# Linear attention and a gated feed-forward block on one core: phi(K) from two values instead of three, first loads split by rows, new orders

## The chip, the core and the metric

The kernel runs on one NeuronCore of one Trainium2 chip. A core has TensorE (PE, matmuls and transposes; its weight loads are shown apart as PEld), VectorE (DVE), ScalarE (ACT), GpSimd (POOL) and SyncE (SP), which here only issues transfers (DMAs). Each engine runs its own instructions in a fixed order; semaphores order them against each other. Matmul results land in PSUM, eight banks of 512 float32 values per partition; everything else is kept in SBUF, 128 partitions.

The metric is the device time of one execution in microseconds, lower is better; the figure of a kernel is the median of several runs.

## The reference

All inputs are bfloat16; 2048 tokens, width 448, 16 heads of 28, inner width 1792.

```python
def _A_ref(x, wqkv, wo):                       # linear attention
    qkv = (x @ wqkv).reshape(B, S, 3, H, Dh).transpose(2, 0, 3, 1, 4)
    q, k, v = qkv[0], qkv[1], qkv[2]
    phi = lambda t: jnp.where(t > 0, t + 1, jnp.exp(t)) + 1e-6
    pq, pk = phi(q), phi(k)
    kv = jnp.einsum("bhsd,bhse->bhde", pk, v)
    z = jnp.einsum("bhsd->bhd", pk)
    num = jnp.einsum("bhqd,bhde->bhqe", pq, kv)
    den = jnp.einsum("bhqd,bhd->bhq", pq, z)[..., None] + 1e-6
    return (num / den).transpose(0, 2, 1, 3).reshape(B, S, D) @ wo

def _B_ref(x, w_gate, w_up, w_down):           # gated feed-forward
    return jnp.einsum("bsf,fd->bsd", _gelu(x @ w_gate) * (x @ w_up), w_down)

h = x + _A_ref(_layernorm(x), A_wqkv, A_wo)
return h + _B_ref(_layernorm(h), B_w_gate, B_w_up, B_w_down)
```

## The kernel before

The 2048 tokens are 16 tiles of 128. Tile t is row t of each partition's 16 consecutive tokens, so tiles 0 and 1 lie next to each other in memory for every partition.

**Stage 1, K and Q (lines 430 to 505).** For each tile VectorE makes the statistics (`bnst1_t`, `bnag1_t`, lines 413 and 414) and ACT the reciprocal deviation (`ln1_t`, `rstd1_t`). Tiles 0 to 3 are normed by VectorE (`normD_t`, line 435), transposed by TensorE (`tr0_t`, `tr1_t`, line 443) and copied out of PSUM in two halves, the first by ACT (`evxA_t`), the second by VectorE (`evxD_t`). Tiles 4 to 15 are normed by GpSimd (`normP_t`) and transposed by a DMA that SP issues (`xT_t`). The normed tile has 512 columns; the last 64 are ones, so the fourth of its four transposed blocks has 64 rows of data and 64 rows of ones. The weights' fourth block is padded with zero rows (line 364) to meet them.

`k_t` is four matmuls of 448 columns (line 469, the helper `proj`). `ek_t` is ACT's exponential of K; `ck_t` (line 481) caps it at 1 + 1e-6; `pk_t` (line 482) adds it to the maximum of K and 1e-6: that is phi(K). `pt4_t` (line 488; for tiles 10 to 15 `pt1_t` and `pt3_t`, one and three matmuls) adds the product of the normed tile and phi(K) up in PSUM banks 4 to 7 over all tiles: kv is later formed from this sum and the V weights, so V itself is never computed. The columns of ones make z in the lower half of bank 7. `q_t` is computed in the same way, with an exponential (`eq_t`) and a relu (`rq_t`) on ACT; `cq_t` and `aq_t` on VectorE finish phi(Q). K and Q share PSUM banks 0 to 3 in the order of `SEQ` (line 245), so that a projection can start when the readers of the fourth one before it are done: Q1 follows K1 in bank 2, K3 follows K0 in bank 1.

**The turn (lines 514 to 555).** `z1` (ACT) and `z0` (VectorE) take z out of PSUM. `evpA_0`, `evpA_1` (ACT) and `evpD_2`, `evpD_3` (VectorE) take the four sums out. `kv` (line 527) multiplies with the V weights, `kvm` masks the heads, `w2_c` (line 547) multiplies with the output weights, so that the attention's output of a tile is one product with `w2`.

**Stage 2 (lines 558 to 708).** Pairs of tiles: phi(Q) times z summed per head (`t1p_t`, `t1d_t`, `dr_t`), division, transpose, `out...`, residual `hr_t`, second norm, transpose. Then chunks of the feed-forward block: `gu..` (lines 731 and 733, gate and up in the two halves of the array), gelu on ACT (`ge..`), product on VectorE (`hm..`), `down..` (line 697) and the last residual.

**Order.** Nothing is reordered while the kernel runs. `ORDERS` lists, engine by engine, the tasks' numbers (a task's number is its place in the program text, counted from 0); `HOLD` says for a task that waits for several others which of the waits is issued first. Waits are derived from the buffers that tasks read and write; a wait that another one implies is dropped. The first loads are issued by SP and ACT (lines 364 to 377), before ACT's first table load; `warm` (line 407) is 40 matmuls of 128 columns on ones, ahead of everything else on TensorE.

The orders before, by names, up to what the prediction steps through:

```text
PE : warm tr0_0 tr1_0 tr0_1 tr1_1 k_0 tr0_2 tr1_2 k_1 q_0 tr0_3 tr1_3 k_2 k_3 pt4_0 q_1 pt4_1 pt4_2 q_2 k_4 ...
     k_14 pt3_10 k_15 pt1_11 pt3_11 pt1_12 pt1_13 pt3_12 pt1_14 pt1_15 pt3_13 pt3_14 pt3_15 q_5 q_4 kv q_7 q_8 w2_2 ...
DVE: wvpad wqkpad bnst1_0 bnag1_0 bnst1_1 bnag1_1 normD_0 bnst1_2 normD_1 bnag1_2 bnst1_3 evxD_0 bnag1_3 normD_2
     evxD_1 normD_3 evxD_2 bnst1_4 ck_0 bnag1_4 bnst1_5 pk_0 bnag1_5 evxD_3 ck_1 bnst1_6 pk_1 ...
     ck_15 pk_15 aq_3 cq_1 evpD_3 z0 aq_1 t1d_0 dr_0 evpD_2 rd_0 dr_1 dr_2 kvm ...
SP : dx0 dx2 dw1 dx4 dw1_t dx8 dx12 dwv dwv_t dwo xT_4 xT_5 xT_6 xT_8 xT_7 ...
ACT: dx1 dw0 dw0_t tbl1 ln1_0 rstd1_0 ln1_1 rstd1_1 evxA_0 ...
```

(`dxN` loads x from tile N, `dw0` the first 384 rows of the K weights, `dw0_t` the last 64, `dw1` and `dw1_t` the Q weights.)

Of the kernel before, what the change touches and what calls it, by code (L numbers as in the profile page):

```python
# [822 lines left out]
```

## Time and profile before

| | us |
|---|---|
| median of 3 runs | 190.3 |
| lowest, highest run | 190.28, 190.66 |
| span of the profiled execution, first to last instruction | 188.3 |

The profiled execution's own time is not given apart from its span; the 2.0 us between the span and the median are taken as what lies around the span.

How to read the rows. A row of a timeline has start and duration in us, the engine, the source line (of this listing), the operation, what it writes and reads, how many instructions are merged, and in brackets the engine's idle time before it and what ended it. A row of a group has count, busy time, mean ns of one, and idle time before. A row of a stage has its ends, its length, each engine's busy time and count, the granted clock, the DMA engines' share and GB/s. A row of a DMA issue has KB and the us from issue to landing; a row of a queue has packets, MB and share. The trace models the end of a matmul: a single one of 448 columns shows 350 ns, though the next can start much earlier, so the spacing of starts tells the pace.

### The profile page before, as it was taken

To read this page: it belongs to the slowest core of one execution; us is meant where nothing else is said; L and a number is where in the kernel's file an instruction comes from. 1 tells how busy PE (TensorE), PEld (TensorE's weight loads), DVE (VectorE), ACT (ScalarE), POOL (GpSimd) and SP (SyncE) were. 2 spreads that over 40 slices of the span, in tenths; PEclk is the share of its full clock that TensorE was granted. 3 is DMA by queue.
4 is the path that set the end of the run, shared out by engine and by line. 5 is a ranking of instruction groups with operands and counts; after the bars stand their busy time and mean duration, and the time that the engine had idled before them with its cause. 6 is when DMAs were issued, how large, how long until landed. Compare 5 with 4: busy or idle time off the path is not lost.

```text
span 188.3 us, 4459 instructions
## 1 busy us (share of the span) xinstructions
PE 184.3 (98%) x1813; PEld 109.2 (58%) x1813; DVE 129.3 (69%) x330; ACT 76.5 (41%) x220; POOL 50.0 (27%) x91
## 2 busy tenths in 40 slices
PE   7999999999999999999999999999999999999994
PEld 7545555555688788965554555555545545454554
DVE  4999959999899998786796762562645244335432
ACT  3878752799963231432234222321242222224100
POOL 6067910704505686033614000206100000000000
PEclk9999999999999999999999999999999999999999
DMA  5996458999393526820005720000096000002024
GB/s 169 387 231 88 96 104 194 218 222 174 65 320 64 95 52 116 84 52 0 0 3 98 144 54 0 0 3 2 3 135 111 3 0 24 3 0 98 3 79 140
DMA packets 35076, 17.11 MB, mean 91 GB/s; under 512 B 26864, under 2 KB 33648, under 8 KB 35056
## 3 DMA queue, kind: packets, MB, share of 16 engines
q1 hardware_dynamic: 34432, 16.32, 41.1%
q10 hardware_dynamic: 624, 0.52, 0.8%
q8 instruction: 14, 0.23, 0.5%
q14 instruction: 6, 0.05, 0.1%
HBM read 8.26 MB, written 1.84 MB: 54 GB/s over the span
## 4 chain that ended last, share of the span: by engine, by line
PE 94%; DVE 3%; DMA 1%; issue 0%
PE ps L733 38%; PE ps L697 19%; PE ps L469 12%; PE ps L731 9%; PE ps L488 6%; PE ps L627 3%; PE ps L678 3%; PE ps L628 2%; DMA x_sb<-in_A_x_dram 1%; DVE st L413 1%; PE ps L617 1%; PE ps L547 1%; PE ps L527 1%; PE ps L443 0%; PE ps L654 0%; DVE den L572 0%
## 5 line engine op out<-in xcount | busy, mean ns | idle before, releaser
L733 PE MATMUL ps<-hnT,wgu_sb 64*128 64x512 bf16 (+1 forms) x490 | 88.8, 333 | 0.0
L731 PE MATMUL ps<-hnT,wgu_sb 64*128 64x512 bf16 (+1 forms) x490 | 88.6, 333 | 0.0
L751 ACT ACTIVATE gl<-ps 128x256 bf16<-128x256 f32 x112 | 36.6, 383 | 85.3 <-PE ps L731 84.4
L753 DVE TENSOR_TENSOR hh<-ps,gl 128x256 bf16<-128x256 f32 x112 | 42.1, 416 | 41.4 <-ACT gl L751 41.3
L733 PEld LDWEIGHTS ps<-hnT,wgu_sb 64*128 64x128 bf16 x490 | 45.2, 94 | 32.9 <-DVE hh L753 3.4
L731 PEld LDWEIGHTS ps<-hnT,wgu_sb 64*128 64x128 bf16 x490 | 45.4, 94 | 2.5
L697 PE MATMUL ps<-wd_sb,hh 64*128 64x448 bf16 x392 | 41.5, 349 | 0.0
L697 PEld LDWEIGHTS ps<-wd_sb,hh 64*128 64x128 bf16 x392 | 23.2, 94 | 14.5
L469 PE MATMUL ps<-wqk_sb,xnT 128*128 128x448 bf16 x128 | 27.4, 353 | 0.0
L413 DVE BATCH_NORM_STATS2 st<-x_sb 128x6 f32<-128x448 bf16 x32 | 19.2, 612 | 1.8 <-DMA x_sb<-in_A_x_dram 1.7
L585 POOL TENSOR_TENSOR t<-pq,zbc 128x448 f32<-128x448 bf16 x12 | 12.3, 1042 | 23.7 <-DVE pq L583 22.0
L469 PEld LDWEIGHTS ps<-wqk_sb,xnT 128*128 128x128 bf16 x128 | 11.9, 98 | 11.4 <-DVE pk L482 0.8
L488 PE MATMUL ps<-pk,xnn 128*128 128x448 bf16 x64 | 13.9, 352 | 0.0
L627 PE MATMUL ps<-w,pqnT 64*128 64x448 bf16 x49 | 11.5, 349 | 0.1
L425 POOL TENSOR_SCALAR ln<-mv 128x2 f32<-128x2 f32 x7 | 2.0, 291 | 35.2 <-DVE mv L414 35.0
L480 ACT ACTIVATE e<-ps 128x448 bf16<-128x448 f32 x16 | 8.5, 539 | 5.6 <-PE ps L469 5.5
L628 PE MATMUL ps<-pt_sb,pqnT 64*128 64x448 bf16 x42 | 10.2, 350 | 0.0
L633 DVE TENSOR_TENSOR x_sb<-ps,x_sb 128x448 bf16<-128x448 f32 x16 | 9.6, 616 | 0.7 <-PE ps L628 0.6
L662 POOL TENSOR_SCALAR hn<-x_sb,nm,rs 128x448 bf16<-128x448 bf16 x14 | 9.9, 719 | 0.4
L482 DVE SCALAR_TENSOR_TENSOR pk<-ps,e 128x448 bf16<-128x448 f32 x16 | 9.8, 617 | 0.1
L488 PEld LDWEIGHTS ps<-pk,xnn 128*128 128x128 bf16 x64 | 6.3, 98 | 5.9 <-DVE pk L482 0.3
L453 POOL TENSOR_SCALAR xnn<-x_sb,nm,rs 128x448 bf16<-128x448 bf16 x12 | 8.9, 744 | 2.2 <-ACT rs L422 1.9
(85 smaller groups left out, 160.5 us busy)
## 6 DMA issues: line engine op xcount, KB each, us to landing
out_dram<-x_sb SPq DMA_DIRECT2D x15, 112.0 KB, 1.8
wd_sb<-in_B_w_down_dram SPq DMA_DIRECT2D x1, 1568.0 KB, 8.4
x_sb<-in_A_x_dram SPq DMA_DIRECT2D x3, 448.0 KB, 5.9
wgu_sb<-in_B_w_gate_dram SPq DMA_DIRECT2D x1, 896.0 KB, 12.1
wgu_sb<-in_B_w_up_dram SPq DMA_DIRECT2D x1, 896.0 KB, 16.5
wgu_sb<-in_B_w_gate_dram SPq DMA_DIRECT2D x1, 672.0 KB, 6.1
wgu_sb<-in_B_w_up_dram SPq DMA_DIRECT2D x1, 672.0 KB, 8.5
wo_sb<-in_A_wo_dram SPq DMA_DIRECT2D x1, 392.0 KB, 7.5
```

The source lines that it names most:

```text
L413: op("dve", lambda e: e.bn_stats(st[:, t, :], src_ap), [b_src], [b_st[t]], "bnst%s_%d" % (tag, t))
L469: ins = e.matmul(ps[:, bk, 0:D], xnT[:, t, k, :], wqk_sb[:, k, c0:c0 + D], start=(k == 0), stop=(k == 3))
L488: ins = e.matmul(ps[:, BK_PT[c], 0:D], xnn[:, t % XN_R, c * 128:(c + 1) * 128], pk[:, ip, :], start=(t == 0), stop=(t == T - 1))
L585: op("pool", lambda e, n=n: e.tensor_tensor(t1[:, n, :], pq[:, a + n, :], zbc[:, :], ALU.mult), [b_pq[a + n]] + b_z, [b_t1[n]], "t1p_%d" % ...
L627: e.matmul(ps[:, BK_OUT[0], 0:D], pqnT[ra, i2, sg // 2, :], w2[ra, sg // 2, :], start=(sg == 0), stop=(sg == 5))
L628: ins = e.matmul(ps[:, BK_OUT[1], 0:D], pqnT[rb, i2, 3 + (sg + 1) // 2, :], (w2 if sg == 6 else w2s)[rb, sg // 2, :], start=(sg == 0), sto ...
L662: op("pool", lambda e, t=t, sh=sh: e.tensor_scalar(hn[:, sh, 0:D], x_sb[:, t, :], nm2[:, t:t + 1], rs2[:, t:t + 1], ALU.add, ALU.mult), [b ...
L697: ins = e.matmul(ps[:, bko[half][n], 0:D], hh[rows, j, sl[n]], wd_sb[rows, j, :], start=(j == 0 and (half == 0 or p == 6)), stop=(j == NJ ...
L731: first = e.matmul(psG[:, jj * N:(jj + 1) * N], wgu_sb[A_, k, j * 128:(j + 1) * 128], hnT[A_, ka_, c0:c0 + N], start=(k == 0), stop=(k == ...
L733: ins = e.matmul(psU[:, jj * N:(jj + 1) * N], wgu_sb[B_, k, j * 128:(j + 1) * 128], hnT[B_, kb_, c0:c0 + N], start=(k == 0), stop=(k == NK ...
L751: G.add("act", lambda e, gi=gi, cs_=cs_, psG=psG: e.activation(gl[:, gi, cs_], psG[:, cs_], AF.Gelu_apprx_tanh), r=[b_ps[BK_G[i]]], w=[b_g ...
L753: op("dve", lambda e, dst=dst, srcU=srcU, srcL=srcL: e.tensor_tensor(dst, srcU, srcL, ALU.mult), [b_ps[BK_U[i]], b_glh], [b_ar[j_][t % HR] ...
```

## The change

- **phi(K).** Row 64 of the fourth block of the K weights, one of the zero rows that meet the ones, becomes 1 (`w1row`), so that the matmuls give K + 1. `ek_t` takes the exponential with bias -1. `ck_t` is gone; `pk_t` takes the minimum of the exponential and 1 and then the maximum with K + 1.
- **The 1e-6 of phi(K).** phi(K) gets a column more that holds 1e-6 (`pkeps`, set once), and the `pt` matmuls have 449 columns, so that 1e-6 times the column sums of the normed tiles is in column 448 of each bank. It is added when the sums are taken out: `ecol` copies two of these columns to SBUF for ACT's evictions, VectorE's evictions read theirs in PSUM. z gets 2048 x 1e-6 as bias.
- **Loads.** Tiles 0 and 1 are loaded together, partitions 0 to 63 by SP and 64 to 127 by ACT; the statistics of both tiles wait for both. `dw0_t` moves from ACT to SP's second place, `dw1` from SP to ACT's third.
- **Warm-up.** 36 matmuls instead of 40.
- **Orders.** All five orders are new and `HOLD` names a first wait for most tasks that wait. 857 tasks instead of 868.

```diff
-    WARM = 40
+    WARM = 36
...
-        pk = sb("pk", [128, PK_R, D], BF16)
+        pk = sb("pk", [128, PK_R, D + 2], BF16)
...
-        dma_x("sp", 0, 1)
-        dma_x("act", 1, 2)
+        op("dve", lambda e: e.memset(wqk_sb[64:65, 3, D:2 * D], 1.0), [b_wpad[0]], [b_w1r], "w1row")
+        x01 = [dma(q, x_sb[rows, 0:2, :], xv[rows, 0:2, :], b_, "dx0%s" % "ab"[i]) for i, (q, rows, b_) in enumerate((("sp", A_, b_x[0:2]), ("act", B_, [_Buf("x01")])))]
+        dma_w1("sp", wqk_sb, D, 2 * D, b_wk, "dw0_t")
+        dma_w3("act", wqk_sb, D, 2 * D, b_wk, "dw0")
         dma_x("sp", 2, 4)
-        dma_w3("act", wqk_sb, D, 2 * D, b_wk, "dw0")
-        tx1 = dma_w1("act", wqk_sb, D, 2 * D, b_wk, "dw0_t")
-        dma_w3("sp", wqk_sb, 0, D, b_wq, "dw1")
+        tx1 = dma_w3("act", wqk_sb, 0, D, b_wq, "dw1")
         dma_x("sp", 4, 8)
...
+        op("pool", lambda e: e.memset(neg1[:], -1.0), [], [b_neg1], "neg1")
+        op("pool", lambda e: e.memset(eps_s[:], S * EPS), [], [b_epss], "epss")
+        op("pool", lambda e: e.memset(pk[:, :, D:D + 2], EPS), [], [b_pke], "pkeps")
...
-            eks.append(act_exp(lambda e: e.activation(e1[:, i, :], psK, AF.Exp), [b_ps[bk]], [b_e1[i]], "ek_%d" % t))
-            op("dve", lambda e: e.tensor_scalar(e1[:, i, :], e1[:, i, :], 1.0 + EPS, 0.0, ALU.min, ALU.max), [b_e1[i]], [b_e1[i]], "ck_%d" % t)
-            op("dve", lambda e: e.scalar_tensor_tensor(pk[:, ip, :], psK, EPS, e1[:, i, :], ALU.max, ALU.add), [b_ps[bk], b_e1[i]], [b_pk[ip]], "pk_%d" % t)
+            eks.append(act_exp(lambda e: e.activation(e1[:, i, :], psK, AF.Exp, bias=neg1[:, 0:1]), [b_ps[bk], b_neg1], [b_e1[i]], "ek_%d" % t))
+            op("dve", lambda e: e.scalar_tensor_tensor(pk[:, ip, 0:D], e1[:, i, :], 1.0, psK, ALU.min, ALU.max), [b_ps[bk], b_e1[i]], [b_pk[ip]], "pk_%d" % t)
...
-                        ins = e.matmul(ps[:, BK_PT[c], 0:D], xnn[:, t % XN_R, c * 128:(c + 1) * 128], pk[:, ip, :], start=(t == 0), stop=(t == T - 1))
+                        ins = e.matmul(ps[:, BK_PT[c], 0:D + 1], xnn[:, t % XN_R, c * 128:(c + 1) * 128], pk[:, ip, 0:D + 1], start=(t == 0), stop=(t == T - 1))
...
-        op("act", lambda e: e.activation(zbc[B_, :], ps[B_, BK_PT[3], 0:D], AF.Identity), [b_ps[BK_PT[3]]], [b_z[1]], "z1")
+        op("dve", lambda e: e.tensor_copy(ecol[:, 0:2], ps[:, BK_PT[0]:BK_PT[0] + 2, D]), [b_ps[BK_PT[0]], b_ps[BK_PT[1]]], [b_ecol], "ecol")
+        op("act", lambda e: e.activation(zbc[B_, :], ps[B_, BK_PT[3], 0:D], AF.Identity, bias=eps_s[B_, 0:1]), [b_ps[BK_PT[3]], b_epss], [b_z[1]], "z1")
...
-                op("act", lambda e, c=c: e.activation(pt_sb[:, c, :], ps[:, BK_PT[c], 0:D], AF.Identity), [b_ps[BK_PT[c]]], [b_pt[c]], "evpA_%d" % c)
+                op("act", lambda e, c=c: e.activation(pt_sb[:, c, :], ps[:, BK_PT[c], 0:D], AF.Identity, bias=ecol[:, c:c + 1]), [b_ps[BK_PT[c]], b_ecol], [b_pt[c]], "evpA_%d" % c)
...
-                op("dve", lambda e, c=c: e.tensor_copy(pt_sb[:, c, :], ps[:, BK_PT[c], 0:D]), [b_ps[BK_PT[c]]], [b_pt[c]], "evpD_%d" % c)
+                op("dve", lambda e, c=c: e.tensor_scalar(pt_sb[:, c, :], ps[:, BK_PT[c], 0:D], ps[:, BK_PT[c], D:D + 1], None, ALU.add), [b_ps[BK_PT[c]]], [b_pt[c]], "evpD_%d" % c)
```

The new orders, by names, in the same places:

```text
PE : warm tr0_0 tr1_0 tr0_1 tr1_1 k_0 k_1 tr0_2 tr1_2 q_0 tr1_3 tr0_3 k_2 q_1 k_3 pt4_0 pt4_1 q_3 k_4 q_2 pt4_2 pt4_3 ...
     k_14 k_15 pt1_10 pt1_11 pt1_12 pt1_13 pt3_10 pt1_14 pt1_15 pt3_11 pt3_12 pt3_13 pt3_14 pt3_15 q_7 q_5 kv q_4 q_9 w2_2 ...
DVE: wqkpad wvpad w1row bnst1_0 bnag1_0 bnst1_1 bnag1_1 normD_0 bnst1_2 normD_1 bnag1_2 evxD_0 bnst1_3 bnag1_3 evxD_1
     normD_2 bnst1_4 normD_3 bnag1_4 evxD_2 bnst1_5 pk_1 bnag1_5 pk_0 evxD_3 bnst1_6 ...
     pk_14 cq_3 pk_15 aq_3 z0 t1d_0 evpD_3 dr_0 ecol dr_1 evpD_2 dr_2 dr_3 rd_1 kvm ...
SP : dx0a dw0_t dx2 dx4 dw1_t dx8 dx12 dwv dwv_t dwo xT_4 xT_5 xT_6 xT_8 xT_7 ...
ACT: dx0b dw0 dw1 tbl1 ln1_0 rstd1_0 ln1_1 rstd1_1 evxA_0 ...
POOL: ones mhalf eps pkeps kvzpad ones2 ptpad neg1 ident powwarm negm1_4 normP_4 ...
```

In the gated stage the orders change in the same way: the same tasks, swapped in places, on TensorE, ACT and VectorE.

More of the change, by code (lines that the diff above doesn't have):

```diff
@@ L15 @@
 ORDERS = (
[33 rows of a table removed]
[33 rows of a table added]
 )
 HOLD = {
-    66: (36,), 141: (140,), 165: (164,), 214: (213,), 216: (215,), 323: (302,), 326: (324,), 431: (340,), 704:
-    (564,), 735: (734,), 781: (672,), 839: (836,), 849: (846,), 854: (852,), 866: (865,),
[78 rows of a table added]
 }
@@ L290, in bass_sequential_preLN__linear_attn_block__glu_gated_geglu__prompt_kernel @@
         eps_d = sb("eps_d", [128, 1], F32)
+        neg1 = sb("neg1", [128, 1], F32)
+        eps_s = sb("eps_s", [128, 1], F32)
+        ecol = sb("ecol", [128, 2], F32)
         rd = sb("rd", [128, 4, H], F32)
@@ L315, in bass_sequential_preLN__linear_attn_block__glu_gated_geglu__prompt_kernel @@
             _Buf(n) for n in ("ident", "ones", "mones", "mtmp", "mask", "eps", "mhalf", "powtmp"))
-        b_epsd = _Buf("epsd")
+        b_epsd, b_epss, b_ecol, b_neg1, b_pke, b_w1r = _Buf("epsd"), _Buf("epss"), _Buf("ecol"), _Buf("neg1"), _Buf("pke"), _Buf("w1r")
         b_st1, b_mv1, b_nm1, b_ln1, b_rs1 = bufs("st1", T), bufs("mv1", T), bufs("nm1", T), bufs("ln1", T), bufs("rs1", T)
@@ L412, in ln_stats @@
         def ln_stats(t, src_ap, b_src, st, mv, b_st, b_mv, tag):
-            op("dve", lambda e: e.bn_stats(st[:, t, :], src_ap), [b_src], [b_st[t]], "bnst%s_%d" % (tag, t))
+            G.add("dve", lambda e: e.bn_stats(st[:, t, :], src_ap), r=[b_src], w=[b_st[t]], name="bnst%s_%d" % (tag, t), sync=x01[1:] if tag == "1" and t < 2 else ())
             op("dve", lambda e: e.bn_aggr(mv[:, t, :], st[:, t, :]), [b_st[t]], [b_mv[t]], "bnag%s_%d" % (tag, t))
@@ L472, in proj_reads @@
         def proj_reads(t, b):
-            return [(b_xnT[t][0], 0), (b_xnT[t][1], 2), (b[0], 0), (b[1], 3), (b_wpad[0], 3)]
+            return [(b_xnT[t][0], 0), (b_xnT[t][1], 2), (b[0], 0), (b[1], 3), (b_wpad[0], 3)] + ([(b_w1r, 3)] if b is b_wk else [])
         def k_tile(t):
@@ L487, in fpt @@
                     for c in cs:
-                        ins = e.matmul(ps[:, BK_PT[c], 0:D], xnn[:, t % XN_R, c * 128:(c + 1) * 128], pk[:, ip, :], start=(t == 0), stop=(t == T - 1))
+                        ins = e.matmul(ps[:, BK_PT[c], 0:D + 1], xnn[:, t % XN_R, c * 128:(c + 1) * 128], pk[:, ip, 0:D + 1], start=(t == 0), stop=(t == T - 1))
                     return ins
-                G.add("pe", fpt, r=[b_xn[t % XN_R], b_ones2, b_pk[ip]], w=[b_ps[BK_PT[c]] for c in cs], name="pt%d_%d" % (len(cs), t))
+                G.add("pe", fpt, r=[b_xn[t % XN_R], b_ones2, b_pke, b_pk[ip]], w=[b_ps[BK_PT[c]] for c in cs], name="pt%d_%d" % (len(cs), t))
         def q_tile(t):
@@ L511, in bass_sequential_preLN__linear_attn_block__glu_gated_geglu__prompt_kernel @@
             dma("sp", wgu_sb[B_, :, cs], B_w_up[:, cs].rearrange("(k p) n -> p k n", p=64), [b_wu[i]], "dwu%d" % i, after=xts[-1:])
-        op("act", lambda e: e.activation(zbc[B_, :], ps[B_, BK_PT[3], 0:D], AF.Identity), [b_ps[BK_PT[3]]], [b_z[1]], "z1")
+        op("dve", lambda e: e.tensor_copy(ecol[:, 0:2], ps[:, BK_PT[0]:BK_PT[0] + 2, D]), [b_ps[BK_PT[0]], b_ps[BK_PT[1]]], [b_ecol], "ecol")
+        op("act", lambda e: e.activation(zbc[B_, :], ps[B_, BK_PT[3], 0:D], AF.Identity, bias=eps_s[B_, 0:1]), [b_ps[BK_PT[3]], b_epss], [b_z[1]], "z1")
         op("dve", lambda e: e.tensor_copy(zbc[A_, :], zbc[B_, :]), [b_z[1]], [b_z[0]], "z0")
-        op("dve", lambda e: e.tensor_copy(pt_sb[A_, 3, :], ps[A_, BK_PT[3], 0:D]), [b_ps[BK_PT[3]]], [b_pt[3]], "evpD_3")
+        op("dve", lambda e: e.tensor_scalar(pt_sb[A_, 3, :], ps[A_, BK_PT[3], 0:D], ps[A_, BK_PT[3], D:D + 1], None, ALU.add), [b_ps[BK_PT[3]]], [b_pt[3]], "evpD_3")
         for c in range(3):
             if c in (0, 1):
-                op("act", lambda e, c=c: e.activation(pt_sb[:, c, :], ps[:, BK_PT[c], 0:D], AF.Identity), [b_ps[BK_PT[c]]], [b_pt[c]], "evpA_%d" % c)
+                op("act", lambda e, c=c: e.activation(pt_sb[:, c, :], ps[:, BK_PT[c], 0:D], AF.Identity, bias=ecol[:, c:c + 1]), [b_ps[BK_PT[c]], b_ecol], [b_pt[c]], "evpA_%d" % c)
             else:
-                op("dve", lambda e, c=c: e.tensor_copy(pt_sb[:, c, :], ps[:, BK_PT[c], 0:D]), [b_ps[BK_PT[c]]], [b_pt[c]], "evpD_%d" % c)
+                op("dve", lambda e, c=c: e.tensor_scalar(pt_sb[:, c, :], ps[:, BK_PT[c], 0:D], ps[:, BK_PT[c], D:D + 1], None, ALU.add), [b_ps[BK_PT[c]]], [b_pt[c]], "evpD_%d" % c)
         def fkv(e):
```

144 rows, old and new, of tables (HOLD, ORDERS) are left out of this document.

## Prediction

> **What bounds the kernel now.** I read the page first (busy time, chain by engine), then TensorE's waits, then the first 14 us engine by engine, where the change puts most of its edits.
>
> ```profile
> span 188.3 us, 4459 instructions
> PE 184.3 (98%) x1813; PEld 109.2 (58%) x1813; DVE 129.3 (69%) x330; ACT 76.5 (41%) x220; POOL 50.0 (27%) x91
> ...
> PE 94%; DVE 3%; DMA 1%; issue 0%
> ```
>
> TensorE is busy for all but 4 us of the span, and 94% of the chain that ended last is its work. Its waits, whole span, and one row of the weight loads' waits (us in total, times, longest):
>
> ```profile
> PE ps L407 <- POOL eps_d L383: 1.0, 1, 1.0
> PE ps L443 <- DVE xnn L435: 0.4, 1, 0.4
> ```
> ```profile
> PEld ps L733 <- DVE hh L753: 3.4, 12, 0.4
> ```
>
> TensorE has no idle time after its second transpose. The weight loads of the gated stage wait 12 times, at most 0.4 us, and none of it reaches a matmul. A "busy" matmul can still hide a stall, so spacing is the better view (start, duration, how many):
>
> ```profile
> 1.05 4.43 PE L407 MATMUL ps<-ones_bf 128*128 128x128 bf16 x40 [1.05 <-POOL eps_d L383]
> 5.29 0.41 PE L443 MATMUL ps<-ident,xnn 128*128 128x128 bf16 x4
> 6.09 0.40 PE L443 MATMUL ps<-ident,xnn 128*128 128x128 bf16 x4 [0.39 <-DVE xnn L435]
> 6.32 1.11 PE L469 MATMUL ps<-wqk_sb,xnT 128*128 128x448 bf16 x4
> ...
> 7.49 1.68 PE L469 MATMUL ps<-wqk_sb,xnT 128*128 128x448 bf16 x8
> ...
> 12.29 1.68 PE L488 MATMUL ps<-pk,xnn 128*128 128x448 bf16 x8
> ```
>
> Eight 448-wide matmuls take 1.68 us with a drain at the end, four take 0.92 where they run freely: 0.189 us each. So tile K0's four (1.11 us) hold a stall of about 0.18 us. Another stands before the matmuls that form kv (rows further down): 0.22 us. All that a new order can win back on TensorE after 6.09 us is about half a microsecond; the rest of a gain would have to be a start before 6.09.
>
> **The clamp that goes.** These groups are of the whole span (count, busy, mean ns):
>
> ```profile
> L482 DVE SCALAR_TENSOR_TENSOR pk<-ps,e 128x448 bf16<-128x448 f32 x16 | 9.8, 617 | 0.1
> ...
> L481 DVE TENSOR_SCALAR e<-e 128x448 bf16<-128x448 bf16 x16 | 4.2, 271 | 2.3 <-ACT e L480 2.2
> ```
>
> Sixteen clamps leave VectorE, 4.2 us; the operation that makes pk keeps its shape and its 617 ns. In that stage TensorE is already at 0.189 us per matmul, so the 4.2 us are worth nothing by themselves; they would count where pk comes late, and there the new order decides (below). The +1 row costs no matmul: the fourth weight block has 128 rows already. The moving side of the 64 phi(K) matmuls grows from 448 to 449 columns: 0.189/448 = 0.42 ns each, +0.03 us in all; were an odd width to cost as much as a 512-wide one, 64 x 0.027 = 1.7 us, but nothing in the trace suggests such a step, so I keep 0.03.
>
> **Small additions.** The row of ones is one more memset on VectorE, which waits 1.73 us for the first x anyway (row further down); without that wait it would cost its own length, less than 0.5 us. GpSimd, 27% busy, has the new memsets before and between its norms. One of its rows (start, duration):
>
> ```profile
> 3.01 0.29 POOL L380 TENSOR_SCALAR_AFFINE_SELECT ident<-ones_bf 128x128 bf16<-128x128 bf16 x1
> ```
>
> The identity, ready at 3.30, is now made behind four more memsets; the first transposes want it at 5.29, so up to 2 us of delay stay hidden. Bias operands in activations that had none: the rows with a bias (ln, den) are no longer than those without, so 0.
>
> **The start: loads.** Now SP issues tile 0, tiles 2-3, the Q weights, tiles 4-7; ACT issues tile 1 and the K weights.
>
> ```profile
> 0.79 0.87 SPq L346 DMA_DIRECT2D x_sb<-in_A_x_dram  x2
> ...
> 1.25 1.01 ACTq L346 DMA_DIRECT2D wqk_sb<-in_A_wqkv_dram  x2
> ...
> 2.18 0.49 SPq L346 DMA_DIRECT2D x_sb<-in_A_x_dram  x1
> ```
> ```profile
> wqk_sb<-in_A_wqkv_dram ACTq DMA_DIRECT2D x1, 336.0 KB, 4.2
> ...
> x_sb<-in_A_x_dram SPq DMA_DIRECT2D x1, 224.0 KB, 3.4
> ...
> x_sb<-in_A_x_dram ACTq DMA_DIRECT2D x1, 112.0 KB, 2.7
> ```
> ```profile
> x_sb<-in_A_x_dram SPq DMA_DIRECT2D x1, 448.0 KB, 5.7
> ```
>
> Tiles 2-3 (issued near 1.22) land at 4.6, the K weights (1.25) at 5.4, tiles 4-7 (2.18) at 7.9. Each queue issues one transfer per 0.45 us. In the changed order SP has the halves of tiles 0-1, then the 56 KB tail of the K weights, and only then tiles 2-3, issued near 1.7 and behind the 336 KB that ACT issues at 1.25; ACT takes the Q weights, which SP issues now at 1.7, as its third. How the two queues share is seen in packets, in 3.25 to 3.75 us and in 4.0 to 4.5 us (q1 is SP, q10 ACT):
>
> ```profile
> q1 hardware_dynamic: 82, 0.14, 79.1%
> q10 hardware_dynamic: 18, 0.02, 9.2%
> ```
> ```profile
> q10 hardware_dynamic: 202, 0.18, 103.1%
> q1 hardware_dynamic: 10, 0.01, 5.6%
> ```
>
> First tiles 2-3 nearly alone, then the K weights nearly alone: transfers are served one after the other, alternating queues, close to the order of issue. So tiles 2-3 now end when 784 KB plus the 56 KB tail are through. The 784 KB landed at 5.4; 0.18 MB per 0.5 us adds 0.15: about 5.57. Bounds: 4.75 if they still go ahead of the K weights, 5.75 with a slow tail. Tiles 4-7 have the same bytes ahead as before: 7.9 again.
>
> [...]
>
> **The start: VectorE and TensorE.** VectorE now (start, duration):
>
> ```profile
> 3.34 0.63 DVE L413 BATCH_NORM_STATS2 st<-x_sb 128x6 f32<-128x448 bf16 x1 [1.73 <-DMA x_sb<-in_A_x_dram]
> ...
> 5.11 0.62 DVE L413 BATCH_NORM_STATS2 st<-x_sb 128x6 f32<-128x448 bf16 x1
> 5.65 0.38 DVE L435 TENSOR_SCALAR xnn<-x_sb,mv,rs 128x448 bf16<-128x448 bf16 x1
> 5.94 0.18 DVE L414 BATCH_NORM_AGGREGATE mv<-st 128x2 f32<-128x6 f32 x1
> 6.03 0.59 DVE L413 BATCH_NORM_STATS2 st<-x_sb 128x6 f32<-128x448 bf16 x1
> 6.54 0.27 DVE L450 COPY xnT<-ps 128x256 bf16<-128x256 bf16 x1
> ```
>
> The statistics of tile 2 (5.11) stand ahead of the norm of tile 1 (5.65), before and after. If tiles 2-3 land at 5.57, that norm moves from 5.65 to 6.14, the transposes of tile 1 from 6.09 to 6.58, K0 from 6.32 to 6.81. (Both halves of tiles 0-1 must land for the first statistics: near 3.5 us, where ACT's 112 KB land now (0.8 + 2.7), instead of 3.3; this hides in the same wait.) The new order copies tile 0's second half (now at 6.54) before the statistics of tile 3, at 6.52, so K0's stall of 0.18 goes. From there on TensorE's new order is K0 (to 7.56), K1 (8.32), transposes (8.54), Q0 (9.30), transposes (9.52), K2 (10.27), Q1, K3, phi(K) of tiles 0 and 1. Q1 needs K1's PSUM bank and so pk of tile 1. VectorE from 6.14 in the new order, by the start-to-start times above: 6.43, copy 6.52, stats 6.72, 7.35, copy 7.44, norm 7.64, stats of tile 4 at 7.94 (just landed), norm 8.46, 8.75, copy 8.84, stats 9.04, pk of tile 1 9.56 to 10.17. Q1 starts at 10.33, K3 ends 11.84, phi(K) of tile 1 starts at 12.60, where it starts at 12.29 now: **+0.31 us** with the same work done. Should tiles 2-3 be in time, pk of tile 1 still hangs on tiles 4-7 (7.9) and the gain is mostly given back at Q1: between +0.1 and +0.25. Only with tiles 4-7 near 7.0 as well does it turn: -0.3.
>
> From there to the end of phi(K) the work on TensorE is the same in another sequence, gapless as now. The transposed tiles of 4 to 15 come through SP's queue, twelve transposes one behind the other, each of 2.7 us to its landing:
>
> ```profile
> 10.31 16.93 SPq L455 DMA_TRANSPOSE xnT<-xnn  x12
> ```
> ```profile
> xnT<-xnn SPq DMA_TRANSPOSE x12, 2.7
> ```
>
> Tile 4's goes out by the shift near 10.7 and lands near 13.4; K4 wants it at 14.1 (12.60 and two times 0.76). If it came as late as that or later, every K behind it would be late by the same.
>
> **The turn to kv.**
>
> ```profile
> 34.23 1.68 PE L469 MATMUL ps<-wqk_sb,xnT 128*128 128x448 bf16 x8
> 35.96 1.03 PE L527 MATMUL ps<-pt_sb,wv_sb 128*112 128x112 bf16 x16
> ```
> ```profile
> 34.76 0.62 DVE L572 TENSOR_REDUCE den<-t 128x16 f32<-128x448 f32 x1
> 35.29 0.61 DVE L521 CAST pt_sb<-ps 128x448 bf16<-128x448 f32 x1
> ```
>
> The Q matmuls end at 34.23 + 8 x 0.189 = 35.74; kv starts at 35.96, behind the cast that ends at 35.90. In the new order VectorE has, behind the last phi(K) (34.4): the new copy of two columns, one reduce, then that cast. Queued behind the copy's wait are those two and, on ACT, both evictions with its bias. The copy is shown nowhere; like the two-wide aggregate it takes 0.17 (bounds 0.14 and 0.61): 34.42 + 0.17 + 0.53 + 0.61 = 35.73, kv at 35.77: **-0.17**; with 0.61 it is +0.27. The other inputs are there: z comes from tile 15's first matmul, which now stands five triples (15 x 0.189 = 2.8 us) ahead of the end instead of three (1.7), so z and GpSimd's product for the reduce come 1.1 us sooner.
>
> **Sum.** +0.31 - 0.17 + 0.03 = +0.17 us on the span of 188.3; with the 2.0 us around it (190.3 - 188.3) the forecast is 190.5. The profiled run gives only its span, so it is set against the median. Its own range, 190.2 to 190.9, is no change as far as this kernel's runs can tell, which is 0.2% (0.4 us).
>
> **Rivals.** (1) Faster: all x lands early enough. K0's stall (0.18), some 0.15 at the transposes and first loads and the kv gap (0.17) are won: 190.3 - 0.5 = 189.8. For it: the halves have fewer, larger packets, and VectorE has one clamp less per tile; against it: tiles 2-3 are now third on SP. (2) Slower: the clock. The 40 warm matmuls run at 0.107 us for 128 columns, and later four transposes of that width take 0.22 us on the chain, 0.055 each:
>
> ```profile
> 7.43 0.22 PE ps L443 x4
> ```
>
> The clock doubled about when the warm run ended. With 36 they end 0.43 us sooner, at 4.9, and TensorE idles before and after the first transposes, longer still if tile 1 is late. If the doubling then fails, work from 6.6 on runs at half speed; a second run-up as long as the warm row would cost half of 4.3, a short one near 0: I take 1.1, so 191.5. It decides at whether 3.9 us of matmuls suffice; the row shows only that 4.3 do. [...] (3) Slower: VectorE in the first gated stage.
>
> ```profile
> 50.00:70.00 20.00, 20.00 (x322) 16.77 (x320) 19.43 (x48) 8.50 (x24) 11.30 (x18) 1.00 0.53 131
> ```
>
> TensorE is busy 20.00 of 20 us there, VectorE 19.43: 0.57 us to spare. All its orders are new; one product placed behind a 1.09 us operation, less the 0.4 that weight loads now absorb, costs 0.7: 191.2. (4) Nothing is gained because the clamp was hidden: that is the forecast's own reason.
>
> **Numbers.** Forecast 0.45, (1) 0.32, (2) 0.10, (3) 0.13. Of the forecast's 0.45 some 0.10 lie over 190.7; of (1) 0.05 within 0.2%. That makes faster 0.27, same 0.40, slower 0.33. The range 189.5 to 191.5 leaves out the far ends of (1) and (2).
>
> **What would show it.** Statistics of tile 2 waiting for x until about 5.6; first transposes of tile 1 near 6.6; no stall inside K0; kv within 0.1 us of the last Q matmul; 0.189 us spacing from there to the end; warm matmuls followed at once by 0.056 us transposes. The forecast is wrong if tile 2 does not wait, if K matmuls show 0.37 us spacing, or if weight loads in 50 to 90 us wait long enough to leave TensorE idle.

## The result, and the profile after

| | before | after |
|---|---|---|
| median of 4 runs each, us | 190.3 | 196.1 |
| lowest, highest | 190.28, 190.66 | 195.68, 196.52 |
| span of the profiled execution | 188.3 | 194.5 |
| ratio, 95% interval | | 1.029 (1.027 to 1.032) |

The change makes the kernel 5.8 us slower: neither the 190.5 that was forecast nor any time in the range. The profiled execution of after is the one of 196.52 us.

One execution of e2 (197.67 us) and the profiled one of e5 (222.46 us) count as slow, so the medians, ranges and ratios below are of the others and nothing is read from the profile of e5.

The page of after: span, busy time, chain by engine, and the groups of phi(K) (count, busy, mean ns, idle before):

```profile
span 194.5 us, 4437 instructions
PE 187.0 (96%) x1809; PEld 137.6 (71%) x1809; DVE 128.0 (66%) x316; ACT 76.8 (40%) x220; POOL 50.5 (26%) x94
...
PE 85%; DVE 6%; DMA 4%; POOL 2%; issue 1%; SPq 1%; ACT 0%
...
L563 DVE SCALAR_TENSOR_TENSOR pk<-e,ps 128x448 bf16<-128x448 bf16 x16 | 9.7, 613 | 5.1 <-ACT e L562 5.1
L562 ACT ACTIVATE e<-ps,neg 128x448 bf16<-128x448 f32 x16 | 9.9, 629 | 6.5 <-PE ps L551 6.2
```

The clamp is gone, and VectorE has 1.3 us less to do. TensorE had 94% of the chain that ended last and has 85%: VectorE, transfers and GpSimd now have a part of it. TensorE's own waits say where (in total, times, longest):

```profile
PE ps L525 <- DVE xnn L517: 2.6, 2, 1.7
PE ps L815 <- DVE hh L835: 1.2, 2, 0.7
...
PE ps L551 <- DMA xnT<-xnn: 0.3, 1, 0.3
```

**The start.** TensorE of after (start, duration, how many):

```profile
1.04 4.02 PE L489 MATMUL ps<-ones_bf 128*128 128x128 bf16 x36 [1.04 <-POOL eps_t L461]
5.97 0.61 PE L525 MATMUL ps<-ident,xnn 128*128 128x128 bf16 x4 [0.91 <-DVE xnn L517]
8.24 0.61 PE L525 MATMUL ps<-ident,xnn 128*128 128x128 bf16 x4 [1.66 <-DVE xnn L517]
8.64 3.19 PE L551 MATMUL ps<-wqk_sb,xnT 128*128 128x448 bf16 x8
...
12.05 1.44 PE L551 MATMUL ps<-wqk_sb,xnT 128*128 128x448 bf16 x4
...
15.82 1.69 PE L569 MATMUL ps<-pk,xnn 128*128 128x449 bf16 x8
```

Two losses. The transposes of tile 1 come at 8.24 where they came at 6.09: 2.15 us. Then TensorE runs at half speed: eight K matmuls take 3.19 us, 0.37 each, where eight took 1.68 before; only from about 13 us on do they run at 0.19. From start to start these eight lose 1.48 us, Q0's four 0.52 and the transposes of tiles 1 and 2 0.36; K0's stall of 0.18 is gone. That is another 2.2. phi(K) of tile 1, whose start was forecast 0.31 later than 12.29, starts at 15.82 + 0.76 = 16.58: 4.29 later. The trace of this execution holds no record of the clock, and its clock column then reads 1.00 throughout, so here the spacing is the witness and the column is not.

Why tile 1 is late is seen on VectorE, on the issues of both queues, and in the packets of 4.5 to 5.4 us (q10 is ACT's queue, q1 SP's):

```profile
4.06 0.63 DVE L495 BATCH_NORM_STATS2 st<-x_sb 128x6 f32<-128x448 bf16 x1 [1.98 <-DMA x_sb<-in_A_x_dram]
...
7.26 0.63 DVE L495 BATCH_NORM_STATS2 st<-x_sb 128x6 f32<-128x448 bf16 x1 [1.34 <-DMA x_sb<-in_A_x_dram]
7.80 0.38 DVE L517 TENSOR_SCALAR xnn<-x_sb,mv,rs 128x448 bf16<-128x448 bf16 x1
```
```profile
0.79 0.59 SPq L425 DMA_DIRECT2D x_sb<-in_A_x_dram  x1
1.43 0.83 SPq L425 DMA_DIRECT2D wqk_sb<-in_A_wqkv_dram  x1
2.32 1.05 SPq L425 DMA_DIRECT2D x_sb<-in_A_x_dram  x2
```
```profile
1.40 1.13 ACTq L425 DMA_DIRECT2D wqk_sb<-in_A_wqkv_dram  x2
```
```profile
q10 hardware_dynamic: 319, 0.28, 90.4%
q1 hardware_dynamic: 35, 0.05, 15.4%
```

The halves of x take 0.56 to 0.59 us to issue and the tail of the K weights 0.83, so tiles 2 and 3 go out at 2.32, behind both of ACT's weight transfers (the two rows of 336 KB begin at 1.40 and 2.02). The Q weights are served first, nearly alone, and x of tile 2 lands at 7.23. (e2 below has an execution with the same loads in which the order of the two is turned, and x lands at 5.96.) VectorE stands at the statistics of tile 2 until 7.26, with the norm of tile 1, whose x has been there since 3.96, queued behind them.

**One late transpose, and the turn to kv.** TensorE of after, around tile 7 and around kv:

```profile
22.65 0.92 PE L551 MATMUL ps<-wqk_sb,xnT 128*128 128x448 bf16 x4
23.90 1.69 PE L551 MATMUL ps<-wqk_sb,xnT 128*128 128x448 bf16 x8 [0.33 <-DMA xnT<-xnn]
...
39.16 1.68 PE L551 MATMUL ps<-wqk_sb,xnT 128*128 128x448 bf16 x8
40.81 1.00 PE L609 MATMUL ps<-pt_sb,wv_sb 128*112 128x112 bf16 x16
```

Four matmuls from 22.65 end their share at 23.41; the next start at 23.90, 0.49 late. kv starts 0.14 behind the Q matmuls (39.16 + 8 x 0.189 = 40.67) where it was 0.22.

**The first gated stage.** VectorE and GpSimd of after:

```profile
61.37 0.75 DVE L835 TENSOR_TENSOR hh<-ps,gl 128x256 bf16<-128x256 f32 x2
62.89 0.33 DVE L746 COPY hn<-hn 128x448 bf16<-128x448 bf16 x1 [0.78 <-POOL hn L744]
...
63.68 0.28 DVE L746 COPY hn<-hn 128x448 bf16<-128x448 bf16 x1
63.87 0.75 DVE L835 TENSOR_TENSOR hh<-ps,gl 128x256 bf16<-128x256 f32 x2
...
79.25 1.45 DVE L665 TENSOR_TENSOR pq<-pq,eq 128x896 bf16<-128x896 bf16 x1
...
80.96 0.77 DVE L746 COPY hn<-hn 128x448 bf16<-128x448 bf16 x1
```
```profile
62.14 1.50 POOL L744 TENSOR_SCALAR hn<-x_sb,nm,rs 128x448 bf16<-128x448 bf16 x2
```

The gate and up matmuls come in groups, numbered in order; each group has two products on VectorE (`hm0_`, `hm1_`), and TensorE can begin a group when the products of the second one before it are done. hn is the output of the second norm. Between two groups' products (61.37 and 63.87) the new order has two copies of GpSimd's hn (`wrap_2`, `wrap_3`). The first waits 0.78 us for GpSimd's hn, which starts at 62.14, and the product that TensorE's group 5 needs waits behind it. At group 11 VectorE waits for nobody: ahead of the products that group needs stand an addition that finishes phi(Q) (`aqP_6`, called a multiply in the expectation of e7), which takes 1.45 us where the six of before take 0.61 in the mean, and a copy (`wrap_5`) of 0.77. No run shows why these two take so long here. Matmul start to matmul start, the two stalls are 0.66 and 0.87 us. In sum 4.3 + 0.5 + 1.5 = 6.3, against 6.2 of span.

### The profile page after: what moved, and what is told of

It reads as the page before. It is cut to its first block, busy times and chain, and to the rows that moved or that the text cites. A ratio compares the mean times of both kernels' runs of the same rounds, so it can differ in the third digit from the quotient of the medians.

```text
span 194.5 us, 4437 instructions
## 1 busy us (share of the span) xinstructions
PE 187.0 (96%) x1809; PEld 137.6 (71%) x1809; DVE 128.0 (66%) x316; ACT 76.8 (40%) x220; POOL 50.5 (26%) x94
## 4 chain that ended last, share of the span: by engine, by line
PE 85%; DVE 6%; DMA 4%; POOL 2%; issue 1%; SPq 1%; ACT 0%
PE ps L815 20%; PE ps L779 19%; PE ps L813 18%; PE ps L551 12%; PE ps L569 5%; PE ps L760 3%; DMA x_sb<-in_A_x_dram 3%; PE ps L709 2%; DMA xnT<-xnn 2%; PE ps L710 2%; DVE hh L835 1%; DVE st L495 1%; POOL rs L508 1%; PE ps L699 1%; DVE pq L665 1%
## 5 line engine op out<-in xcount | busy, mean ns | idle before, releaser
L779 PE MATMUL ps<-wd_sb,hh 64*128 64x448 bf16 x392 | 40.4, 349 | 0.0
L779 PEld LDWEIGHTS ps<-wd_sb,hh 64*128 64x128 bf16 x392 | 32.1, 94 | 5.5
L551 PE MATMUL ps<-wqk_sb,xnT 128*128 128x448 bf16 x128 | 29.2, 371 | 0.3 <-DMA xnT<-xnn 0.3
L551 PEld LDWEIGHTS ps<-wqk_sb,xnT 128*128 128x128 bf16 x128 | 12.8, 102 | 12.8 <-issue 1.4
L569 PE MATMUL ps<-pk,xnn 128*128 128x449 bf16 x64 | 13.7, 353 | 0.0
L563 DVE SCALAR_TENSOR_TENSOR pk<-e,ps 128x448 bf16<-128x448 bf16 x16 | 9.7, 613 | 5.1 <-ACT e L562 5.1
L562 ACT ACTIVATE e<-ps,neg 128x448 bf16<-128x448 f32 x16 | 9.9, 629 | 6.5 <-PE ps L551 6.2
## 6 DMA issues: line engine op xcount, KB each, us to landing
wgu_sb<-in_B_w_up_dram SPq DMA_DIRECT2D x1, 896.0 KB, 15.2
```

The lines of the kernel that those rows point to most:

```text
L551: ins = e.matmul(ps[:, bk, 0:D], xnT[:, t, k, :], wqk_sb[:, k, c0:c0 + D], start=(k == 0), stop=(k == 3))
L569: ins = e.matmul(ps[:, BK_PT[c], 0:D + 1], xnn[:, t % XN_R, c * 128:(c + 1) * 128], pk[:, ip, 0:D + 1], start=(t == 0), stop=(t == T - 1))
L779: ins = e.matmul(ps[:, bko[half][n], 0:D], hh[rows, j, sl[n]], wd_sb[rows, j, :], start=(j == 0 and (half == 0 or p == 6)), stop=(j == NJ ...
```

## The experiments

Each time is a median beside runs of the kernel before on the same chip; the ratio is to those. P^T in the expectations is the sum that the `pt` matmuls add up.

**e1, e2: the warm-up alone,** in the kernel before (e1) and in after (e2).

```diff
-    WARM = 40
+    WARM = 36
```
```diff
-    WARM = 36
+    WARM = 40
```

> The kernel before with 36 warm matmuls instead of 40, nothing else. Theory A (36 matmuls are too few for the clock to double): the K matmuls after 6.3 us show 0.373 us spacing until some 9 to 13 us, time 191.3 to 192.5. Theory B (36 are enough as long as TensorE's real work follows soon; the changed kernel's clock stayed low because tiles 2-3 came late and left TensorE idle from 4.9 to 8.2 us): 0.189 us spacing from the first K matmul, 190.3 within 0.3.

Measured: 190.63 us, ratio 1.001 (0.9996 to 1.0024). 36 matmuls are enough for the kernel before: the row of its first transposes is

```profile
5.31 0.40 PE L443 MATMUL ps<-ident,xnn 128*128 128x128 bf16 x4 [0.24 <-DVE xnn L435]
```

At half speed, in the profile of after, four of them take 0.61.

> The changed kernel with 40 warm matmuls. Theory A: the clock doubles near 5.3 us as before, K matmuls at 0.189 us from 8.6 on, 2.1 us won: 194.0. Theory B: TensorE still idles from 5.3 to 8.2 us; if that alone keeps the clock low, nothing is won: 196.1 within 0.4.

Measured: 196.0 us (194.08 to 196.55), ratio 1.026 (1.020 to 1.033). Forty do not mend after, but its runs spread over 2.5 us. The profiled one is the fastest, with a span of 192.1 us:

```profile
1.43 0.57 SPq L425 DMA_DIRECT2D wqk_sb<-in_A_wqkv_dram  x1
2.06 1.05 SPq L425 DMA_DIRECT2D x_sb<-in_A_x_dram  x2
```
```profile
7.23 1.68 PE L551 MATMUL ps<-wqk_sb,xnT 128*128 128x448 bf16 x8
```

Two things differ from the profile of after, with the same loads in the same order. The tail of the K weights takes 0.57 us to issue and not 0.83, while ACT's first weight issue takes 0.87 and not 0.59. So x of tiles 2 and 3 goes out at 2.06, now ahead of the Q weights (2.30), and lands at 5.96 instead of 7.23; the transposes of tile 1 come at 7.00. And the clock, which is full from 4.64 on (the four transposes at 5.65 take 0.40), stays full. The other two runs (196.0 and 196.55) have a mean granted clock of 0.991 (1 is full speed), so there it was not full throughout; they were not profiled, and where their x landed is not known.

**e3, e4: after with the loads of before** (e4 with 40 warm-up matmuls as well).

```diff
-        x01 = [dma(q, x_sb[rows, 0:2, :], ...) ...]
-        dma_w1("sp", wqk_sb, D, 2 * D, b_wk, "dw0_t")
+        dma_x("sp", 0, 1)
+        dma_x("act", 1, 2)
+        dma_x("sp", 2, 4)
         dma_w3("act", wqk_sb, D, 2 * D, b_wk, "dw0")
-        dma_x("sp", 2, 4)
-        tx1 = dma_w3("act", wqk_sb, 0, D, b_wq, "dw1")
+        dma_w3("sp", wqk_sb, 0, D, b_wq, "dw1")
+        tx1 = dma_w1("act", wqk_sb, D, 2 * D, b_wk, "dw0_t")
```

> The changed kernel with the first loads of the kernel before (tile 0 on SP, tile 1 on ACT, tiles 2-3 second on SP, the K tail and the Q weights back in their places), 36 warm matmuls. Both theories: the first transposes of tile 1 back near 6.1 us (from 8.2). Theory A: the clock still comes late, 2.1 us won: 194.0. Theory B: start and clock are both mended, 4.3 us won: 191.8, and what is left is the two stalls in the gated stage (1.4 us) and 0.2.

> The changed kernel with the loads and the 40 warm matmuls of the kernel before; phi(K) and the orders stay new. Both theories: 4.3 us won, 191.8, the rest being the two stalls of TensorE in the gated stage, which then belong to the new orders; if those stalls came only from the late start, 190.3.

Measured: 193.37 us, ratio 1.0148 (1.0121 to 1.0174), and 193.34, ratio 1.0156 (1.0124 to 1.0189). The loads are worth 2.7 us of the 5.8; some 3.0 stay, with or without the four matmuls, twice what e4's forecast and theory B of e3 left. Of e4, the wait at K4 and TensorE's waits in the gated stage:

```profile
15.07 1.69 PE L552 MATMUL ps<-wqk_sb,xnT 128*128 128x448 bf16 x8 [0.93 <-DMA xnT<-xnn]
```
```profile
PE ps L816 <- DVE hh L836: 1.2, 2, 0.7
```

K4 waits 1.1 us for its transposed tile, Q1 0.3 for pk of tile 1, and the gated stage has the same two stalls (0.64 and 0.85 from start to start). That is the 2.9 us; in after, where all starts later, the late transposed tile costs 0.5 and Q1 nothing.

**e5: before with the loads of after.** The diff of e3 the other way round.

> The kernel before with nothing but the loads of after (x of tiles 0 and 1 in two halves of 64 partitions on two queues, tiles 2 and 3 third on SP, the K tail second on SP, the Q weights third on ACT's queue); 40 warm-up matmuls as before. Theory L (the loads cost about 2.8 of the 5.8 us, through tiles 2 and 3 landing at 7.2 in place of 4.8, and through the clock that doubles late when the warm-up is followed by idle time): 192.5 to 194.5, tile 2's x landing at 6.0 to 7.3 and the transposes of tile 1 at 7.5 or later. Rival (the split costs nothing by itself, the new orders are what cannot stand it): within 0.5 us of the kernel before.

Measured: 193.59 us (193.27 to 194.81), ratio 1.016 (1.011 to 1.021): theory L. The loads cost 3.1 us in the kernel before as well, so the loss does not come from their meeting the new orders. Where x landed in these runs is not known.

**e6, e9: phi(K) alone,** with loads, warm-up and orders of before (`HOLD` stays that of after, in e12 too); they differ in the place of the copy of the two columns.

```diff
 DVE, e6: ... aq_3 cq_1 ecol evpD_3 z0 aq_1 t1d_0 dr_0 evpD_2 rd_0 ...
 DVE, e9: ... aq_3 cq_1 evpD_3 z0 aq_1 t1d_0 ecol evpD_2 dr_0 rd_0 ...
```

> The kernel after with the loads, the 40 warm-up matmuls and the instruction orders of before: of the change only phi(K) is left (the clamp gone, exp with a bias, the added one in the weight row, the corrections of P^T). Theory O (the 3.0 us that were left with the loads of before are the new orders: 0.3 at Q1, 1.1 at K4, 1.5 at two places of the gated stage): 190.0 to 190.7. Rival P (the arithmetic costs by itself: exp is 0.09 us longer, 16 times 0.09 is 1.4 on ScalarE, and it is on the way of the K tiles): 191 to 192.5, with waits for ScalarE between 10 and 40 us. Rival G (the missing clamp frees VectorE): below 189.9.

Measured: 193.98 us, ratio 1.0167 (1.0141 to 1.0192), which looks like the rival. But no wait is for ScalarE. `ecol` reads the first two sums, which the last phi(K) matmuls still write; placed ahead of `evpD_3`, it holds VectorE for 2.03 us, and kv waits. Stage rows of e6 (ends, length, busy PE, PEld, DVE, ACT, POOL, then the granted clock):

```profile
37.00:38.00 1.00, 0.00 (x0) 0.00 (x0) 1.00 (x3) 0.57 (x2) 1.00 (x2) 1.00 1.08 217
...
39.00:40.00 1.00, 1.00 (x6) 0.41 (x4) 1.00 (x5) 0.54 (x3) 0.75 (x1) 0.59 1.07 238
...
42.00:43.00 1.00, 1.00 (x5) 0.50 (x4) 0.32 (x1) 0.00 (x0) 0.00 (x0) 0.70 1.03 207
```

TensorE idles for 2 us and then, already busy again, runs at half clock from 39.18 to 42.60 (0.59 and 0.70 are the mixed slices): a second price for one wait. This price was of my placing of `ecol`, and not of the arithmetic; e9 shows the arithmetic.

> phi(K) of the change alone, with loads, warm-up and orders of before, as in the run named phi with old orders, but with the copy of the two correction columns (ecol) behind the first of Q's products with z instead of ahead of the copy of P^T's last part, where it waited for the last P^T matmuls and held VectorE for 2.03 us. Theory O (the arithmetic itself is worth nothing either way): the stall of 2.1 us ahead of kv and the half-speed matmuls behind it go, which is 194.0 less 3.4: 190.3 to 190.9. Rival P (the correction of P^T by columns costs the turn to kv in any order): a stall of 0.6 us or more ahead of kv, and 191.2 or more.

Measured: 190.8 us, ratio 1.0027 (1.0008 to 1.0046). phi(K) itself costs 0.5 us (0.2 to 0.9): no gain from the clamp, and no loss to speak of. kv stands 0.4 behind the Q matmuls, and K4, 0.77 late in the profiled run, waits once more for its transposed tile (the last section has a possible reason):

```profile
PE ps L524 <- DMA xnT<-xnn: 0.6, 1, 0.6
PE ps L582 <- DVE den L627: 0.2, 1, 0.2
```

**e7, e8: e4 with the orders mended by hand.**

```diff
 DVE, both  : -hm0_2 wrap_2 hr_5 wrap_3 hm0_3 hm1_3 hr_4
              +hm0_2 hr_5 hm0_3 hm1_3 wrap_2 wrap_3 hr_4
              -wrap_6 aqP_6 hm1_9 wrap_5 hm0_9 hm0_10 wrap_7 hm1_10
              +wrap_6 hm1_9 hm0_9 wrap_5 wrap_7 aqP_6 hm0_10 hm1_10
 PE, e8 only: -q_0 tr1_3 tr0_3 k_2 q_1 k_3 pt4_0 pt4_1 q_3 k_4 q_2 pt4_2 pt4_3 k_5
              +q_0 tr0_3 tr1_3 k_2 k_3 pt4_0 q_1 pt4_1 q_3 q_2 pt4_2 k_4 pt4_3 k_5
 DVE, e8 too: pk_0 ahead of pk_1
```

> The kernel after with loads and 40 warm-up matmuls of before, and with one thing more changed, VectorE's order in the first gated stage at two places: the copies of hn of tiles 2 and 3 stand behind the two products of group 3, and those of tile 5 and 7 and a multiply by Q's exponential behind the two products of group 9. Theory O: the two stalls of TensorE there (0.64 and 0.85 us) go, so 193.3 less 1.5 is 191.8 (191.5 to 192.3). Rival (VectorE has too much work there in any order, and the stall comes back at a later group): 192.8 to 193.4, with stalls of the same sum elsewhere between 54 and 80 us.

Measured: 192.87 us, ratio 1.0107 (1.0077 to 1.0137): 0.9 us better than e4 by the ratios, not 1.5, and in the range of the rival. The stalls at groups 5 and 11 are gone from there, but others came, one behind a transfer of the attention's output and one smaller at a product (TensorE's waits of e7):

```profile
PE ps L682 <- DMA pqnT<-pqn: 0.6, 1, 0.6
PE ps L788 <- DVE hh L808: 0.4, 1, 0.4
```

> As the run before it, and the order of the first tiles mended too: K4 stands behind Q3, Q2 and the P^T of tile 2 (with the kernel before's order of K2, K3, P^T 0, Q1), and phi(K) of tile 0 ahead of that of tile 1 on VectorE. Theory O: the stalls at Q1 (0.3) and K4 (1.1) go too: 191.8 less 1.2 is 190.6 (190.1 to 191.0), the same as the kernel before. Rival (xT of tile 4, which is a transfer that lands at 15.0, is late for any order that has tile 4 in the first 15 us): 191.2 to 191.9, the wait for xT of tile 4 showing at its new place.

Measured: 194.48 us, ratio 1.0198 (1.0159 to 1.0237): worse than e7 and outside the ranges of both theories, a plain miss. TensorE's order was changed and ScalarE's was not, so TensorE now waits for ScalarE's work on Q (0.7), for pk (0.4) and for a transposed tile (0.5):

```profile
PE ps L524 <- ACT eq L550: 0.7, 1, 0.7
PE ps L524 <- DMA xnT<-xnn: 0.5, 1, 0.5
```

**e12: the orders of before up to the gated stage, those of after from there.** e9, with every engine's list cut at the first task of the gated stage and continued in the order of after.

```diff
 DVE: -hm1_2 hm0_2 cqP_7 hr_4 hm1_3 hm0_3 hr_5 wrap_3 ... aqP_7 wrap_2
      +hm1_2 hm0_2 wrap_2 hr_5 wrap_3 hm0_3 hm1_3 hr_4 ...
 (and all that follows, on all five engines)
```

> As phi with old orders and ecol later (loads, warm-up and orders of before), but from the first product of the gated stage on every engine follows the order of after, unmended. Theory O (of the 2.9 us that stay with the loads of before, the order of VectorE in the first gated stage is 1.5: two stalls of 0.64 and 0.85 of TensorE behind products that wait for copies of GpSimd's hn): 191.9 to 192.6, with the two stalls at the groups 5 and 11. Rival (the stalls in that stage follow from what the first 50 us leave late, and not from the order there): 190.5 to 191.2, with no stall over 0.4 between 52 and 82 us.

Measured: 192.41 us, ratio 1.0085 (1.0067 to 1.0104), with the two stalls at groups 5 and 11 and nothing else new:

```profile
PE ps L788 <- DVE hh L808: 1.3, 2, 0.7
```

The stalls belong to the order in that stage, and not to what the first 50 us leave late. By the steps between the ratios of e9, e12, e4 and after, 0.0294 of 190.3 us, or 5.6, divide into phi(K) 0.5, order of the gated stage 1.1, order of the first 50 us 1.4 and loads 2.6 (0.0027, 0.0058, 0.0071 and 0.0138); with the intervals of two ratios in each step, these are good to half a microsecond or somewhat more.

**e10, e11: what it is about the loads.** e10 is before with the split loads (e5), but x of tiles 2 and 3 second on SP; its diff is against e5. e11 is after with its own loads, but tile 1's work ahead of tile 2's.

```diff
 e10 : x01 = [... halves of tiles 0, 1 ...]
-        dma_w1("sp", wqk_sb, D, 2 * D, b_wk, "dw0_t")
+        dma_x("sp", 2, 4)
...
-        dma_x("sp", 2, 4)
+        dma_w1("sp", wqk_sb, D, 2 * D, b_wk, "dw0_t")
 e11, DVE: -normD_0 bnst1_2 normD_1 bnag1_2 evxD_0 bnst1_3 bnag1_3 evxD_1 normD_2
           +normD_0 normD_1 evxD_0 evxD_1 bnst1_2 bnag1_2 bnst1_3 bnag1_3 normD_2
 e11, ACT: -evxA_0 ln1_2 evxA_1     +evxA_0 evxA_1 ln1_2
```

> The kernel before with the split loads, but x of tiles 2 and 3 second on SP's queue and the K tail third. Theory L1 (the split is harmless; the loss is the place of tiles 2 and 3 in the queue): they land at 4.9 to 5.7 in place of 7.3, the transposes of tile 1 come at 6.5 to 6.9 in place of 8.3, the clock doubles before 8; 190.8 to 191.9. Theory L2 (the halves of 64 partitions, that land 0.6 later than whole tiles did, are a loss by themselves, or the K tail, now late, holds K0): 192.5 or more.

Measured: 193.17 us (191.05 to 193.53), ratio 1.0117 (1.0071 to 1.0163): the median is in the range of theory L2, one run in that of L1, and the profile has some of both. The place counts: tile 2's x lands at 6.09, where in after it landed at 7.23, and the wait of its statistics is 0.28. But the split counts too: SP's first two issues take 1.46 us where the same two of before took 0.87, and the transposes of tile 1 come at 7.10. Behind two idle stretches of nearly 1 us each, the clock falls (rows as for e6):

```profile
6.00:7.00 1.00, 0.29 (x4) 0.11 (x3) 0.88 (x3) 0.50 (x2) 0.00 (x0) 1.00 0.99 374
7.00:8.00 1.00, 0.88 (x7) 0.45 (x8) 1.00 (x6) 0.80 (x4) 0.00 (x0) 0.94 1.06 350
8.00:9.00 1.00, 1.00 (x6) 0.54 (x6) 0.80 (x3) 0.60 (x3) 0.00 (x0) 0.50 1.02 373
...
11.00:12.00 1.00, 1.00 (x9) 0.59 (x8) 0.50 (x2) 0.72 (x4) 0.17 (x1) 0.85 1.18 224
```

That fall is most of the loss: the run of 191.05 us has a mean clock of 1.000, the three of 192.88 to 193.53 have 0.991. Where the clock holds, the split costs some 0.6 us in this place, by that one run.

> The kernel after, its loads and 36 warm-up matmuls included, with one change of order at the start: on VectorE the normalization of tile 1 and the copies of the transposes of tiles 0 and 1 stand ahead of the statistics of tile 2, and on ScalarE the copy of tile 1's transposes ahead of tile 2's logarithm. Theory W (the late x of tiles 2 and 3 costs through VectorE's order: tile 1, whose x is there at 3.96, is queued behind statistics that wait for tile 2's x until 7.26): tile 1's transposes at 6.7 in place of 8.24, K0 at 7.0 in place of 8.64, the clock doubled before 11 in place of 12.9; 192.9 to 194.6. Rival X (what counts is when tiles 2 and 3 are there; K0 and K1 only run earlier and TensorE then waits for tile 2): 195.4 to 196.4, with a wait of over 1 us ahead of tile 2's transposes or Q0.

Measured: 194.21 us (194.13 to 194.28), ratio 1.0194 (1.0181 to 1.0208): theory W, 1.9 us of after's loss taken back by order alone, with x as late as in after.

```profile
6.61 0.40 PE L497 MATMUL ps<-ident,xnn 128*128 128x128 bf16 x4 [0.32 <-DVE xnn L489]
6.84 1.68 PE L523 MATMUL ps<-wqk_sb,xnT 128*128 128x448 bf16 x8
9.25 0.40 PE L497 MATMUL ps<-ident,xnn 128*128 128x128 bf16 x4 [0.73 <-DVE xnn L489]
```

Tile 1's transposes come at 6.61, K0 and K1 run at full speed, and TensorE waits 0.9 us (from start to start) for tile 2. The two profiles differ in one thing more: here the clock is full at the first transposes (5.89, four in 0.40), before the orders part, and in after it was not (5.97, 0.61). What carries the 1.9 us is that all four runs lie within 0.15 of each other; how much of it the clock makes is open. No version that was run beats the kernel before; of those with the new phi(K), e9 comes nearest.

## Why the prediction was wrong, point by point

- **TensorE sets the end: right, and more than was meant.** With 98% busy there was half a microsecond to win and any stall to lose. Of the three stretches that lose, two stood in the prediction as rivals of 0.10 and 0.13.
- **The clamp is worth nothing: right** (e9). 449 columns: eight matmuls take 1.69 for 1.68, right. "Bias operands ... so 0": wrong in size, the exponential takes 629 ns, where the row of before has

```profile
L480 ACT ACTIVATE e<-ps 128x448 bf16<-128x448 f32 x16 | 8.5, 539 | 5.6 <-PE ps L469 5.5
```

  The 16 x 0.09 = 1.4 us lie on ScalarE, which is 40% busy, and e9 bounds what of it reaches the end.
- **"The start: loads" is the step that failed.** It had "each queue issues one transfer per 0.45 us", tiles 2 and 3 "issued near 1.7" and landing at 5.57, at most 5.75. They were issued at 2.32, since the issues before them took 0.59 and 0.83 us, and landed at 7.23. By the rule used, whole transfers in order of issue, read from the packets of before in two half microseconds, the Q weights (2.02) come first once the true issue times are put in. The profile of e2 bears that out: with the same loads, x out at 2.06 and the Q weights at 2.30, x was there at 5.96. The bounds were about how two queues share, and the issue time, which decided the order, had none. The rule itself is not strict: in e2 the queues had 69 and 78 packets in 4.5 to 5.0 us, where in after they had 35 and 319 in 4.5 to 5.4, and x landed ahead of the K weights (6.4) that were issued at 1.40. These counts are all that the runs show of how the queues share. The halves of tiles 0 and 1 came later as well: the second was in place at 3.96 where whole tiles landed at 3.3 and 3.5.
- **VectorE's order at the start: right.** Norm of tile 1 behind the statistics of tile 2, 0.54 behind their start: 7.26, 7.80. e11 shows that this order, and not the late x alone, made it cost 1.9 us. The prediction saw the queue and took it as given.
- **"Gapless as now" behind the start: wrong, the clock.** Rival (2) had the half speed, and named the idle time, but put the four matmuls first: 36 do as well as 40 where x is in time (e1), and what goes with the loss is the idle time behind them (0.91 and 1.66 us), which the late x makes. Its sign, 0.37 us spacing, came. Its price was 1.1; the half speed made 2.2.
- **The transposed tiles of SP's queue: mis-sized.** "2.7 us to its landing" was a median. The first ones took up to 5.0 (below), and the new order has K4 one group of four matmuls earlier: 1.1 us in e4. In after itself all starts later and K7 pays 0.5.
- **The turn to kv: right.** -0.17 forecast (its own 35.77 for kv makes -0.19), -0.08 came; the copy of two columns takes 0.16 for 0.17.
- **Rival (3), the gated stage: the place right, half of the cause, and half of the price.** It had 0.7 once, for a product behind a long operation. That came at group 11 (0.87, behind operations of 1.45 and 0.77). At group 5 what stands ahead is a short copy that waits 0.78 us for GpSimd (0.66): 1.5 in all. From 19.43 of 20 us busy it read "0.57 us to spare"; where instructions run in a fixed order, a late input of one of them counts too.
- **The rivals were taken as alternatives.** Slow loads (with the clock behind them) and the gated order come from separate edits, and their losses added up. The forecast's 0.45 asked that none of them go wrong.
